# Another order of exponentials and maxima, and work moved away from four places, in a four-layer attention kernel

## The chip, the cores and the metric

The kernel runs on one core of a Trainium2 chip. The core has five engines, each with an instruction stream of its own: TensorE (PE; its weight loads are listed as PEld), VectorE (DVE), ScalarE (ACT), GpSimd (POOL) and SyncE (SP, which here only issues DMAs). Matmul results go to PSUM, which has eight banks of 128 partitions x 512 fp32. The metric is the device time of one execution in microseconds. The kernel before takes 1696.86 us (median of 3 runs, 1695.87 to 1697.17).

## The reference

The input x has 2048 rows of 640. Four layers follow one another in the order A, B, A, B, each with a layernorm ahead of it and a residual around it; both A layers share their weights, and so do both B layers. There are 32 heads of 20. A is linear attention over all rows. B works on four segments of 512 rows: causal softmax attention inside a segment, mixed per head with a read of a memory that earlier segments have filled.

```python
def _A_ref(x, wqkv, wo):
    q, k, v = ...                                   # heads of 20
    phi = lambda t: jnp.where(t > 0, t + 1, jnp.exp(t)) + 1e-6
    pq, pk = phi(q), phi(k)
    kv = jnp.einsum("bhsd,bhse->bhde", pk, v)
    z = jnp.einsum("bhsd->bhd", pk)
    num = jnp.einsum("bhqd,bhde->bhqe", pq, kv)
    den = jnp.einsum("bhqd,bhd->bhq", pq, z)[..., None] + 1e-6
    o = num / den
    return (...)(o) @ wo

def _B_ref(x, wq, wk, wv, wo, beta):
    for s in range(N):                              # 4 segments of 512
        logits = jnp.einsum("bhqd,bhkd->bhqk", qs, ks) * scale + mask
        p = _softmax(logits, axis=-1)
        a_dot = jnp.einsum("bhqk,bhkd->bhqd", p, vs)
        pq = phi(qs)
        num = jnp.einsum("bhld,bhde->bhle", pq, M)
        den = jnp.einsum("bhld,bhd->bhl", pq, z)[..., None] + 1e-6
        a_mem = num / den
        o = g * a_mem + (1.0 - g) * a_dot
        M = M + jnp.einsum("bhld,bhle->bhde", phi(ks), vs)
        z = z + jnp.einsum("bhld->bhd", phi(ks))
    return (...)(o) @ wo
```

## The kernel before, in words

**Two streams.** `run` steps two generators. The dense stream does layernorms, projections, the sums of A and the outputs, for a segment of 512 rows at a time in tiles of 128 rows. The attention stream does the softmax attention of the B layers. Whichever has the lower cost so far goes next. PE executes its instructions in the order in which this program writes them (`MANUAL`). ACT, DVE and POOL are put in order by a scheduler: by priority, which falls as the program goes on and can be raised or lowered for a block (`high_priority`), and with added edges (`issue_after`) that keep an instruction behind another one. Each engine then runs in that order and stops at the first instruction whose inputs are not there.

**Attention.** A unit is four heads of a segment; there are 32 units in a B layer and 64 in all. Every unit passes through three stretches (`STRETCHES`), and a stretch works on up to three units at once: the newest, the one before and the one before that. An entry is an operation, its number and which of these units it belongs to. `max` 0 to 4 (`row_max`) multiplies queries by keys for two banks, after which DVE (L1021) takes the row maxima of each and writes them to `mg`; the banks are free only when DVE is through. `split` turns `mg` into two rows of fp16 (L1030, L1031) that later join the queries, so that the maximum is subtracted by the matmul. `exp` 0 to 4 (`scores`) multiplies keys by queries with those rows for two banks; ACT exponentiates each (L1060, into `pe`) and POOL cuts the causal triangle (L1067). `sum` (`weigh`, L1083) multiplies the exponentials by the values. All of these, and the dense stream too, take their PSUM banks in turn from the same eight.

**The dense stream, where the change touches it.** `opening` starts layer 1: it loads four tiles of x, takes their moments (L350 to L360: statistics on DVE, the power on POOL, `nb` on DVE), normalizes them on ACT (`normed`, L386) and transposes them (`turn`: PE L331, then the lower part through ACT L335 and the upper through DVE L336), while the weights are split into two fp16 parts each (`w_prep`: ACT L271, DVE L272). The weights of the B layers are prepared during layer 1 too; the last of them, `w_Bo`, beside the merge. The merge is the end of the sums of A: DVE scales (L671, L674), PE multiplies (L692), and `wm`, the merged output weight, is formed from L698 to L732. `open_b` opens the buffers of the attention and sets the constant `one` (L841). `a_head` begins the second half of A for a segment (`p_load` reads tiles `pqi` back, `p_read` multiplies and sums them: L764 to L771); `a_second` finishes it, makes the residual x, its moments and the transposed tiles for B. Its `tail` is done later, beside the first value projections of `b_project` (L414, emptied on ACT by `v_half`, L445). `b_out` multiplies by the output weight of B, adds the residual and stores a tile of 128 rows (L982).

```python
L59  [("out", 0, 2), ("exp", 0, 1), ("exp", 1, 1), ("max", 3, 0)],
L60  [("exp", 2, 1), ("exp", 3, 1), ("max", 4, 0), ("split", 0, 0), ("load", 0, 0)]]
```

The other functions named here, and all others that the change touches, follow with their line numbers.

## Time and profile before

| what | value |
|---|---|
| median of 3 runs | 1696.86 us |
| profiled execution | 1699.81 us |
| its span, first to last instruction | 1698.1 us |
| PE busy | 1641.3 us, 97% |
| DVE busy | 1264.6 us, 74% |
| ACT busy | 995.1 us, 59% |
| POOL busy | 505.9 us, 30% |
| PE waiting for DVE's maxima (L1015 for `mg`) | 3.5 us, 6 times |
| DVE waiting for PE before a maximum (L1021) | 41.6 us, 51 times |

The profile is one execution. Its rows come in several views. The page gives each engine's busy time. The view of waits gives an instruction that waited, what it waited for, the total in us, the number of times and the longest. The timeline gives start, duration, engine, line, operation, output <- inputs, shapes and count, and in square brackets the idle time ahead and what ended it. The windows give, for a stretch of time, its length, then the busy time and instructions of PE, weight loads, DVE, ACT and POOL, the mean clock granted to PE (1.00 is full), the share of the DMA engines and their GB/s. Busy times of an engine are no critical path: what ends last in a place is read from the idle times there.

### The profile page before, as it was taken

How to read it: one execution, taken by the hardware profiler on the slowest of the kernel's cores; microseconds unless marked ns; L12 is line 12 of the kernel's file. 1: busy time of each engine (PE TensorE's matmuls, PEld its weight loads, DVE VectorE, ACT ScalarE, POOL GpSimd, SP SyncE). 2: the span in 40 equal slices, each digit the busy share in tenths (PEclk: the TensorE clock that was granted, in tenths of full speed). 3: DMA queues.
4: the chain of work that ended last, by engine and by line, in shares of the span. 5: the costliest groups of instructions: out<-in, count | busy, mean ns of one | idle time of the engine just before them, and what ended most of it. 6: DMA issues, size and time to landing. Idle time of an engine off the chain costs nothing. (4 is left out here: it accounts for less than half of the span.)

```text
span 1698.1 us, 37894 instructions
## 1 busy us (share of the span) xinstructions
PE 1641.3 (97%) x13818; PEld 1021.1 (60%) x13818; DVE 1264.6 (74%) x4015; ACT 995.1 (59%) x1888; POOL 505.9 (30%) x1046
## 2 busy tenths in 40 slices
PE   8999989999999999999999999999999999999998
PEld 6767767564565566556556777766546546645555
DVE  7788886497887787768864566938888888777773
ACT  6666543357657656667665554433675675666763
POOL 4442232022223423433342211210322332232542
PEclk9999999999999999999999999999999999999999
DMA  6415563422312331461211303533232333323422
GB/s 219 156 57 184 214 246 119 148 87 78 114 68 70 127 111 60 134 206 51 80 45 48 108 32 124 191 97 119 76 111 82 104 100 102 106 83 111 148 87 95
DMA packets 110371, 190.99 MB, mean 112 GB/s; under 512 B 14172, under 2 KB 69596, under 8 KB 107624
## 3 DMA queue, kind: packets, MB, share of 16 engines
q1 hardware_dynamic: 97704, 142.68, 26.0%
q0 software_dynamic: 3264, 24.91, 4.1%
q10 hardware_dynamic: 9216, 20.98, 3.2%
q8 instruction: 109, 1.79, 0.4%
q14 instruction: 78, 0.64, 0.1%
HBM read 109.32 MB, written 78.64 MB: 111 GB/s over the span
## 5 line engine op out<-in xcount | busy, mean ns | idle before, releaser
L1021 DVE CUSTOM_DVE_ANT_0 ps<-ps,maskw 128x512 f32<-128x512 f32 (+3 forms) x1024 | 472.1, 521 | 43.8 <-PE ps L1015 41.6
L1060 ACT ACTIVATE pe<-ps,lsc 128x512 f32<-128x512 f32 x640 | 396.7, 696 | 84.5 <-PE ps L1056 82.7
L1067 POOL TENSOR_SCALAR_AFFINE_SELECT pe<-pe 128x256 f32<-128x256 f32 (+1 forms) x640 | 233.3, 372 | 387.6 <-ACT pe L1060 379.6
L414 PEld LDWEIGHTS <-xT 128*128 128x128 f16 x2880 | 280.3, 98 | 112.5 <-issue 6.2
L414 PEld LDWEIGHTS <-oT 128*128 128x128 f16 x1920 | 185.5, 98 | 82.3 <-issue 6.8
L1083 PE MATMUL ps<-pe,v 128*32 128x512 f32 (+3 forms) x2048 | 166.4, 436 | 7.8 <-POOL pe L1067 2.2
L414 PE MATMUL ps<-w_Bo,oT 128*128 128x320 f16 x960 | 143.5, 302 | 3.6 <-ACT oT L335 2.0
L1021 DVE DVE_READ_ACCUMULATOR2_ANT mg<- 128x1 f32 x1024 | 145.2, 142 | 0.0
L590 PE MATMUL ps<-pk,xs 128*128 128x321 f16 (+1 forms) x960 | 138.4, 302 | 4.2 <-DVE pk L553 2.0
L399 PE MATMUL ps<-xT,w_Bq 128*128 128x512 f16 x600 | 140.9, 380 | 1.3 <-ACT pe L1060 0.8
L414 PE MATMUL ps<-wm,oT 128*128 128x320 f16 x960 | 141.0, 299 | 0.5
L414 PE MATMUL ps<-w_Ak,xT 128*128 128x320 f16 x960 | 139.0, 300 | 2.3 <-DVE xT L336 1.6
L414 PE MATMUL ps<-w_Bv,xT 128*128 128x320 f16 x960 | 139.3, 299 | 1.9 <-ACT v L445 1.8
L399 PE MATMUL ps<-xT,w_Bk 128*128 128x512 f16 x600 | 138.5, 379 | 1.2 <-ACT pe L1060 1.2
L414 PE MATMUL ps<-w_Aq,xT 128*128 128x320 f16 x960 | 137.6, 299 | 0.0
L1015 PE MATMUL ps<-ks,qs 60*128 60x512 f16 (+3 forms) x1024 | 123.1, 298 | 8.5 <-DVE mg L1021 3.5
L590 PEld LDWEIGHTS <-xs 128*128 128x128 f16 x960 | 93.2, 98 | 43.6 <-DVE pk L553 2.6
L431 DVE SCALAR_TENSOR_TENSOR e<-e,r 128x320 f32<-128x320 f32 x128 | 67.9, 531 | 67.3 <-ACT r L430 66.9
L1083 PEld LDWEIGHTS ps<-pe,v 128*32 128x32 f32 x2048 | 64.7, 109 | 74.8 <-issue 45.0
L1056 PE MATMUL ps<-qs,ks 62*128 62x128 f16 (+3 forms) x1024 | 105.2, 300 | 1.1 <-ACT pe L1060 1.1
L851 DVE SCALAR_TENSOR_TENSOR nat<-ps,nat 128x512 f16<-128x512 f32 x80 | 55.2, 690 | 64.2 <-ACT nat L850 63.8
L399 PEld LDWEIGHTS <-w_Bk 128*128 128x128 f16 x600 | 57.0, 98 | 66.3 <-issue 6.2
(202 smaller groups left out, 2367.6 us busy)
## 6 DMA issues: line engine op xcount, KB each, us to landing
x<-xn ACTq DMA_DIRECT2D x48, 320.0 KB
qs<-qd SPq DMA_DIRECT2D x128, 120.0 KB
ks<-kd SPq DMA_DIRECT2D x128, 120.0 KB
xo<-x SPq DMA_DIRECT2D x48, 320.0 KB
pqi<-pqd SPq DMA_DIRECT2D x32, 320.0 KB
qd<-nat SPq DMA_DIRECT2D x40, 256.0 KB
kd<-nat SPq DMA_DIRECT2D x40, 256.0 KB
x<-in_A_x SPq DMA_DIRECT2D x16, 320.0 KB
```

The costliest lines, as they stand in the source:

```text
L399: nc.tensor.matmul(p, w[:, c, a, t * P:(t + 1) * P], xT[:, c, b, :], start=k == 0, stop=k == 3 * C - 1)
L414: nc.tensor.matmul(p, xT[:, c, a, i * P:(i + 1) * P], w[:, c, b, n * HN:(n + 1) * HN], start=k == 0, stop=k == 3 * C - 1)
L431: nc.vector.scalar_tensor_tensor(e, e, 1.0, r, op0=OP.min, op1=OP.add)
L590: nc.tensor.matmul(p, xs[:, i, a, c * P:(c + 1) * P], pk[i][:, b, cols], start=i == 0 and a == b, stop=i == NT - 1 and a == 1)
L851: nc.vector.scalar_tensor_tensor(nat[:, 1], p, QK_SHIFT, nat[:, 0], op0=OP.mult, op1=OP.subtract)
L1015: nc.tensor.matmul(bs[par][:, a:a + n], qs[r, p, i * P:(i + 1) * P], ks[r, p, :n], start=True, stop=True)
L1021: nc.vector.tensor_tensor_reduce(bs[par][:, a:a + n], bs[par][:, a:a + n], self.maskw[:, SEG - n:], 1.0, NEG, OP.add, OP.max, G["mg"][:, p ...
L1056: nc.tensor.matmul(b[:, a:a + n], ks[r, p, j * P:(j + 1) * P], qs[r, p, j * P:], start=True, stop=True)
L1060: nc.scalar.activation(e, b, AF.Exp, scale=self.lsc)
L1067: nc.gpsimd.affine_select(d, d, pattern=pat, compare_op=OP.is_ge, fill=0.0, base=0, channel_multiplier=-1)
L1083: nc.tensor.matmul(G["pv"][32 * h4:32 * h4 + 32, j * P:], v[j][:, h * E1:h * E1 + 32], G.pop((p, par, j)), start=j == 0, stop=j == 2, skip ...
```

## The change

It has eight parts.

1. In `STRETCHES`, `max` 3 moves between `exp` 0 and `exp` 1, and `max` 4 with `split` between `exp` 2 and `exp` 3.
2. `exp` 4 gets a higher priority, which counts for ACT and POOL.
3. The DVE half of the split of `w_Bo` gets a lower priority.
4. The constant `one`, and so the buffers of the attention, come after an instruction of the merge (`L["split"]`).
5. In `tail`, the last tile's shift and normalization are written behind the whole first step of the turn before it, and ordered behind the last `v_half` (`self.spread`) as well.
6. In `a_head`, for segments after the first, the load of a tile `pqi` is written one tile ahead of its use.
7. In `opening`, the shift (L355 and L360: `rs`, `nb`) of the last two tiles is ordered behind the lower evacuation of the tile before.
8. The very last tile of the output is stored in two halves of 320 columns.

```diff
-             [("out", 0, 2), ("exp", 0, 1), ("exp", 1, 1), ("max", 3, 0)],
-             [("exp", 2, 1), ("exp", 3, 1), ("max", 4, 0), ("split", 0, 0), ("load", 0, 0)]]
+             [("out", 0, 2), ("exp", 0, 1), ("max", 3, 0), ("exp", 1, 1)],
+             [("exp", 2, 1), ("max", 4, 0), ("split", 0, 0), ("exp", 3, 1), ("load", 0, 0)]]
...
-                self.last = nc.vector.scalar_tensor_tensor(w[:, c, 1, cols], st[:, c, cols], scl, w[:, c, 0, cols],
-                                                           op0=OP.mult, op1=OP.subtract)
+                with self.tc.high_priority(offset=-400) if key == ("B", "o") else nullcontext():
+                    self.last = nc.vector.scalar_tensor_tensor(w[:, c, 1, cols], st[:, c, cols], scl, w[:, c, 0, cols],
+                                                               op0=OP.mult, op1=OP.subtract)
...
-        self.nc.scalar.activation(vv[:, n * HB:(n + 1) * HB, :DH],
-                                  p.rearrange("p (h e) -> p h e", e=DH), AF.Copy, scale=V_SHIFT)
+        self.spread = self.nc.scalar.activation(vv[:, n * HB:(n + 1) * HB, :DH],
+                                                p.rearrange("p (h e) -> p h e", e=DH), AF.Copy, scale=V_SHIFT)
...
-        pq = L["pre"] if s == 0 else [None] * 3
+        pq = L["pre"] if s == 0 else [self.p_load(L, s, 0)]
         box["oT"].append(self.new_oT())
         for i in range(3):
-            yield from self.p_read(L, s, i, box["o"], pq[i])
+            if s > 0 and i < 2:
+                pq.append(self.p_load(L, s, i + 1))
+            yield from self.p_read(L, s, i, box["o"], pq[i], self.nc.vector if s > 0 else None)
...
             t = self.turn(xh[NT - 2], xT, NT - 2)
             yield next(t)
-            with self.tc.issue_after(self.lower.ins):
-                m2 = self.shift(*m)
-            xh.append(self.normed(*m2))
-            yield from t
+            cost = next(t)
+            with self.tc.issue_after(self.lower.ins), self.tc.issue_after(self.spread.ins):
+                xh.append(self.normed(*self.shift(*m)))
+            yield cost
             yield from self.turn(xh[NT - 1], xT, NT - 1)
...
-    def open_b(self):
+    def open_b(self, L):
         self.bp = self.ctx.enter_context(self.tc.tile_pool(name="attn", bufs=1))
-        with self.tc.high_priority():
+        with self.tc.high_priority(), self.tc.issue_after(L["split"].ins):
             self.open_stacks()
...
+                split = st.get("ends") and i == NT - 1
+                if split:
+                    c = slice(n * HN, (n + 1) * HN)
+                    self.q_x.dma_start(dst[s * SEG + i * P:s * SEG + i * P + P, c], xn[:, c])
                 yield self.COST_N
             r = s * SEG + i * P
-            self.q_x.dma_start(dst[r:r + P], xn)
+            if not split:
+                self.q_x.dma_start(dst[r:r + P], xn)
...
                     elif op == "exp":
-                        for bank in EXPS[k]:
-                            self.scores(G, bank)
+                        with self.tc.high_priority(offset=200) if k == 4 else nullcontext():
+                            for bank in EXPS[k]:
+                                self.scores(G, bank)
...
-            m += [self.moments(x[i]) for i in range(2, NT)]
+            m += [self.moments(x[i], False) for i in range(2, NT)]
...
             for i in range(1, NT):
+                if i > 1:
+                    with self.tc.issue_after(self.lower.ins):
+                        m[i - 1] = self.shift(*m[i - 1])
                 xh.append(self.normed(*m[i - 1]))
```

Line numbers of the changed kernel are 1 to 12 higher than those of the one before. How the change moves instructions is shown at three places.

DVE at the first merge. Before, four splits of `w_Bo` stand among the scalings of the merge:

```order
L669 TENSOR_SCALAR eps<-v_83,k_scl 128x1
L272 SCALAR_TENSOR_TENSOR w_Bo<-stage,scl_Bo,w_Bo 128x640 x4
L674 TENSOR_TENSOR xT<-ge,xT 128x320 x2
L671 SCALAR_TENSOR_TENSOR ge<-v_83,eps,rz 128x320
L669 TENSOR_SCALAR eps<-v_84,k_scl 128x1
L669 TENSOR_SCALAR eps<-g_last,k_scl 128x1
L671 SCALAR_TENSOR_TENSOR ge<-v_84,eps,rz 128x320
L674 TENSOR_TENSOR xT<-ge,xT 128x320
```

The fifth follows a little later, and so does the memset of `one` (L841). In the changed kernel, one split stands between the last three L675 (L674 before) of the merge, and the others here, among the instructions that form `wm`:

```order
L770 TENSOR_SCALAR rca<-rca 128x32
L273 SCALAR_TENSOR_TENSOR w_Bo<-stage,scl_Bo,w_Bo 128x640
L771 RECIPROCAL rca<-rca 128x32
L733 SCALAR_TENSOR_TENSOR wm<-ps,wm 128x320 x2
L273 SCALAR_TENSOR_TENSOR w_Bo<-stage,scl_Bo,w_Bo 128x640
L733 SCALAR_TENSOR_TENSOR wm<-ps,wm 128x320 x2
L273 SCALAR_TENSOR_TENSOR w_Bo<-stage,scl_Bo,w_Bo 128x640
L733 SCALAR_TENSOR_TENSOR wm<-ps,wm 128x320 x2
L273 SCALAR_TENSOR_TENSOR w_Bo<-stage,scl_Bo,w_Bo 128x640
L733 SCALAR_TENSOR_TENSOR wm<-ps,wm 128x320
L844 MEMSET one 2x1024
L733 SCALAR_TENSOR_TENSOR wm<-ps,wm 128x320
```

Four splits and the memset have moved from ahead of the merge's last scalings to between the `wm` instructions.

ACT in the opening. Before, the last two tiles are normalized one right behind the other (L386 x2):

```order
L386 ACTIVATE xh<-x,nb,rs 128x640 x2
L428 ACTIVATE e<-ps,inv_Ak 128x320
L430 ACTIVATE r<-ps,inv_Ak 128x320
L335 ACTIVATE xT<-ps 128x3x128
L335 ACTIVATE xT<-ps 128x2x128
L566 ACTIVATE pk<-e,k_scl 128x320
L497 ACTIVATE xs<-xh 128x640
L335 ACTIVATE xT<-ps 128x3x128
```

After the change (line numbers one higher):

```order
L387 ACTIVATE xh<-x,nb,rs 128x640
L429 ACTIVATE e<-ps,inv_Ak 128x320
L431 ACTIVATE r<-ps,inv_Ak 128x320
L336 ACTIVATE xT<-ps 128x3x128
L336 ACTIVATE xT<-ps 128x2x128
L567 ACTIVATE pk<-e,k_scl 128x320
L498 ACTIVATE xs<-xh 128x640
L387 ACTIVATE xh<-x,nb,rs 128x640
L336 ACTIVATE xT<-ps 128x3x128
```

The second normalization has moved behind six instructions of the tile before.

DVE in the third stretch of a unit, beside `p_read`. Here the maxima (each an ISA row that reduces and one that reads the result into `mg`) stand before behind the multiply of `pqi`:

```order
L894 TENSOR_TENSOR acc<-ps,acc 128x63
L336 TENSOR_TENSOR oT<-ps,oT 128x3x128
L749 TENSOR_TENSOR mem_80<-acc,blk 32x2x63
L764 TENSOR_TENSOR pqi<-pqi,z 128x640
L1021 ISA ps,mg<-ps,maskw 128x256
L1021 ISA mg 128x1
L1021 ISA ps,mg<-ps,maskw 128x256
L1021 ISA mg 128x1
```

After the change (L764 is L765 there, L1021 is L1029):

```order
L337 TENSOR_TENSOR oT<-ps,oT 128x3x128
L750 TENSOR_TENSOR mem_80<-acc,blk 32x2x63
L1029 ISA ps,mg<-ps,maskw 128x256
L1029 ISA mg 128x1
L1029 ISA ps,mg<-ps,maskw 128x256
L1029 ISA mg 128x1
L1029 ISA ps,mg<-ps,maskw 128x256
L1029 ISA mg 128x1
L1029 ISA ps,mg<-ps,maskw 128x256
L1029 ISA mg 128x1
L765 TENSOR_TENSOR pqi<-pqi,z 128x640
```

The multiply has moved behind the four maxima of `max` 4.

More of the change, by code (lines that the diff above doesn't have):

```diff
@@ L755, in p_load, with p_read @@
         return pq
-    def p_read(self, L, s, i, o, pq=None):
+    def p_read(self, L, s, i, o, pq=None, eng=None):
         nc = self.nc
-        eng = nc.gpsimd
+        eng = eng or nc.gpsimd
         if pq is None:
@@ L1271, in dense @@
         stage_ctx.close()
-        self.open_b()
+        self.open_b(L)
         i = 0
```

## The prediction

> **What bounds the kernel now.** I read the page first: which engine fills the span, and at what clock.
>
> ```profile
> span 1698.1 us, 37894 instructions
> PE 1641.3 (97%) x13818; PEld 1021.1 (60%) x13818; DVE 1264.6 (74%) x4015; ACT 995.1 (59%) x1888; POOL 505.9 (30%) x1046
> ```
>
> TensorE (PE) is the bound. The change removes no matmul, so all it can win is PE's idle time, 1698.1 − 1641.3 = 56.8 us, and time at half clock. The next view is therefore the waits of PE by what ended them (total us, times, longest):
>
> ```profile
> PE ps L1015 <- DVE mg L1021: 3.5, 6, 0.8
> ...
> PE ps L692 <- DVE xT L674: 2.3, 5, 0.6
> ...
> PE ps L1083 <- POOL pe L1067: 2.2, 7, 0.6
> ...
> PE ps L399 <- ACT pe L1060: 2.0, 5, 0.4
> PE ps L1015 <- ACT pe L1060: 2.0, 5, 0.6
> ...
> PE ps L414 <- ACT v L445: 1.8, 2, 0.9
> PE ps L414 <- DVE xT L336: 1.6, 1, 1.6
> ```
>
> The idle time is in many small pieces, so each part of the change can win a few us at most. The profiled execution took 1699.81 us, 1.71 more than its span; the median of the runs is 1696.86, 2.95 lower. I sum against 1699.81 and carry the difference over to the median.
>
> **The first merge (weight splits L272, `one` L841).** The windows compare the first merge (layer 1) with the second (layer 3), then the phase behind the first that forms `wm`. Columns: length, then busy time and instructions of PE, weight loads, DVE, ACT, POOL, then the clock.
>
> ```profile
> 233.30:247.90 14.60, 10.38 (x107) 8.52 (x105) 14.38 (x39) 6.38 (x15) 1.80 (x6) 0.81 0.61 232
> 1070.40:1077.20 6.80, 6.80 (x108) 6.20 (x106) 6.72 (x19) 3.86 (x10) 0.92 (x3) 1.00 0.19 56
> 247.90:257.70 9.80, 9.80 (x80) 5.33 (x78) 7.19 (x20) 4.02 (x11) 4.84 (x5) 0.94 0.77 276
> ```
>
> In the first merge DVE is busy 14.38 of 14.60 us: it is the bound there, not PE. The timeline shows what stands on DVE beside the merge:
>
> ```profile
> 228.91 3.26 DVE L272 SCALAR_TENSOR_TENSOR w_Bo<-stage,scl_Bo,w_Bo 128x640 f16<-128x640 f32 x4
> ...
> 236.13 0.88 DVE L272 SCALAR_TENSOR_TENSOR w_Bo<-stage,scl_Bo,w_Bo 128x640 f16<-128x640 f32 x1
> ...
> 237.63 0.91 DVE L841 MEMSET one<- 2x1024 f16 x1
> ```
>
> In the new order one L272 stays ahead of the last two L674 and four go between the L732 of the `wm` phase, with the memset ahead of the last. So 4 x 0.82 (3.26/4) + 0.91 = 4.2 us leave the merge, which ends that much earlier. In the `wm` phase DVE then has 7.19 + 4.2 = 11.4 us of work for a stretch of 9.80: 1.6 us come back, since the matmuls behind need the last `wm`. Net −2.6; ends −4.2 (all of it finds room) and 0 (all comes back).
>
> The clock bears on this place and on the opening. Windows of 3.4 us, busy PE and clock as above:
>
> ```profile
> 17.10:20.50 3.40, 3.01 (x19) 1.67 (x17) 3.40 (x10) 3.36 (x8) 0.00 (x0) 1.00 0.30 122
> 20.50:23.90 3.40, 1.49 (x10) 0.90 (x11) 2.43 (x11) 3.17 (x7) 2.69 (x5) 0.99 1.06 358
> 23.90:27.30 3.40, 3.40 (x16) 2.66 (x15) 1.60 (x4) 2.28 (x6) 2.35 (x8) 0.50 0.61 211
> 27.30:30.70 3.40, 3.40 (x27) 2.54 (x26) 2.02 (x5) 2.67 (x7) 2.20 (x2) 1.00 0.91 293
> ```
>
> ```profile
> 239.00:242.40 3.40, 1.78 (x27) 1.26 (x26) 3.40 (x9) 1.92 (x4) 1.08 (x4) 0.99 0.75 312
> 242.40:245.80 3.40, 2.32 (x20) 1.95 (x20) 3.33 (x10) 2.62 (x7) 0.34 (x1) 0.50 0.85 265
> 245.80:249.20 3.40, 3.40 (x25) 2.87 (x24) 2.42 (x8) 0.44 (x2) 1.14 (x4) 0.51 0.96 391
> ```
>
> A window with PE busy 1.49, 1.78 or 2.32 us is followed by one at half clock; one with 3.01 or 3.40 is not. In 245.8–249.2 PE is full at half clock, so without that dip up to 1.7 us more would go. PE's work in the merge would be spread over some 10.4 instead of 14.6 us, near 2.4 us a window, too close to 2.32 to count on; I leave the 1.7 to a rival. The Trainium skill ("TensorE: Matmul & The Clock Gate", What's actually happening) says the clock halves after an idle window of about 3.4 us and returns after a busy one, in windows that run free of the kernel. The half clock and the return agree with the trace; that the window must be idle does not, since 1.49 busy us were enough. By the page no dip would be left to lose or to win here, and the sum would lack the opening's 1.7 us below.
>
> **The opening (moments of the last two tiles).** PE waits 1.63 us for DVE's L336, ahead of which two `nb` (L360) wait for POOL:
>
> ```profile
> 21.55 0.21 DVE L360 TENSOR_SCALAR nb<-mv,rs 128x1 f32<-128x1 f32 x1 [0.44 <-POOL rs L355]
> ...
> 22.77 1.73 ACT L386 ACTIVATE xh<-x,nb,rs 128x640 f32<-128x640 f32 x2
> 22.86 2.72 PE L414 MATMUL ps<-w_Ak,xT 128*128 128x320 f16 x13 [1.63 <-DVE xT L336]
> ...
> 25.37 1.92 PE L331 MATMUL ps<-ident,xh 128*128 128x128 f32 x8
> 25.61 0.53 ACT L428 ACTIVATE e<-ps,inv_Ak 128x320 f32<-128x320 f32 x1 [1.12 <-PE ps L414]
> ...
> 27.08 2.30 PE L414 MATMUL ps<-w_Ak,xT 128*128 128x320 f16 x15
> ...
> 27.59 0.72 ACT L497 ACTIVATE xs<-xh 128x640 f16<-128x640 f32 x1
> ```
>
> The change takes the `nb`, their waits and so some 0.65 us (0.44 + 0.21) away from L336. L414 then runs mostly ahead of 23.9, where the clock halves, and its 13 end some 1.5 us earlier. But the L386 of the last tile, now side by side with the one before (x2 at 22.77), goes behind six ACT instructions, L428 to L497, which take 28.31 − 25.61 = 2.7 us. From 24.1 (25.61 − 1.5) that makes 26.8, and with its own 0.87 (half of 1.73) 27.7; I say 28.0, since the L335 among the six wait for transposes at half clock. PE's transposes of both tiles follow one another (L331 x8), so the last three wait for it, and L414 starts about 28.35: +1.3. In 23.9–27.3 PE would then be busy about 1.9 us, less than 2.32, and the next window falls to half clock: another 1.7. I take +2.0, because some of that dip would stand beside waits; ends −0.7 (only L336 counts) and +3.0.
>
> **The tail of a segment.** A PE wait of 0.92 stands at 1193.43, its twin of 0.93 in the first B layer (the row of 1.8 us, 2 times, above):
>
> ```profile
> 1192.14 0.92 ACT L386 ACTIVATE xh<-xn,nb,rs 128x640 f32<-128x640 f32 x1 [0.75 <-DVE nb L360]
> ...
> 1192.96 0.42 ACT L445 ACTIVATE v<-ps 128x320 f32<-128x320 f32 x1
> ...
> 1193.43 1.79 PE L414 MATMUL ps<-w_Bv,xT 128*128 128x320 f16 x12 [0.92 <-ACT v L445]
> ```
>
> ACT waits 0.75 for `nb`, normalizes for 0.92, and only then empties the bank that PE needs. Behind the change L445 comes first, so both waits go: −1.8. Late next is the normalized tile itself, some 1 us later; its transposes stand behind a dozen L414 (1.79 us), which cover most of it; I give back 0.4. Taken −1.4; ends −1.8 and +0.5.
>
> **Exponential 4 first on ACT.** Its two activations now stand together and ahead of evacuations that stood before or between them. The longest of the seven waits of L1083 for POOL:
>
> ```profile
> 902.31 0.57 ACT L430 ACTIVATE r<-ps,inv_Ak 128x320 f32<-128x320 f32 x1
> ...
> 902.72 1.31 ACT L1060 ACTIVATE pe<-ps,lsc 128x512 f32<-128x512 f32 x2
> ...
> 904.24 0.99 PE L1083 MATMUL ps<-pe,v 128*32 128x256 f32 x8 [0.63 <-POOL pe L1067]
> ```
>
> L430 goes behind, so 0.41 (902.72 − 902.31) of the 0.63 goes here. Of the 2.2 us in all I count a little over half: −1.2; ends −2.2 and +1.5, since `r` comes 1.3 us later in some units, and DVE's L431 behind it, though no matmul is near (taken at 0).
>
> **Maxima between the exponentials.** On DVE the four maxima of stretch 3 now stand ahead of the multiply L764, which waits for a DMA:
>
> ```profile
> 1264.62 0.92 DVE L764 TENSOR_TENSOR pqi<-pqi,z 128x640 f32<-128x640 f32 x1 [0.94 <-DMA pqi<-pqd]
> ...
> 1266.76 1.03 PE L1015 MATMUL ps<-ks,qs 60*128 60x512 f16 x5 [0.63 <-DVE mg L1021]
> ```
>
> The other such place has 1.21 of DVE and 0.80 of PE. Both PE waits should go: −1.4. Elsewhere the maxima reach PE one pair of exponentials earlier (128 places, two in each of 64 units) and that pair as much later. How long a pair is, and how DVE stands to PE:
>
> ```profile
> 362.56 0.61 PE L1056 MATMUL ps<-qs,ks 62*128 62x384 f16 x8
> ```
>
> ```profile
> DVE ps L1021 <- PE ps L1015: 41.6, 51, 3.3
> ```
>
> The eight matmuls are two pairs, so 0.3 us each. Only 51 times did DVE wait for PE before a maximum; mostly it is behind, and a maximum that comes 0.3 us early meets its bank that much less free. Against it, ACT gets four activations in two bursts instead of one, and PE's waits for `pe` (2.0 + 2.0 above) lie where ACT is behind. I set these two against each other: taken −1.5 for the whole part; ends −4 (those waits gone as well) and +10 (the first rival). The new order of the loads of `pqi` on SP's queue differs at two places only: 0.
>
> **The end.** The last output leaves in two halves:
>
> ```profile
> 1694.35 0.55 DVE L493 SCALAR_TENSOR_TENSOR xn<-ps,ioB,xo 128x320 f32<-128x320 f32 x1 [1.49 <-PE ps L414]
> ```
>
> DVE ends at 1694.90, the span at 1698.1: 3.2 us of issue, packets and closing. Only packets shrink, by half: −0.4; ends −0.8 and 0 (one more issue).
>
> Sum: −2.6 + 2.0 − 1.4 − 1.2 − 1.5 − 0.4 = −5.1. 1699.81 − 5.1 = 1694.7 in a profiled execution, and 1696.86 − 5.1 = 1691.8 as a median (−0.30%). What a measurement of this kernel tells from no change is about 0.2%, 3.4 us.
>
> **Rivals.**
> - Slower: the maxima come too early for their banks. At 0.3 us a place, a quarter of the 128 places costs 32 x 0.3 = 9.6 us. The other parts give −3.6, so 1696.9 − 3.6 + 9.6 = 1702.9. It decides for slower from 23 places on (7.0/0.3). For it: DVE is mostly behind PE. Against: only 3.5 us of waits for `mg` today, in 6 places, and PE was only 0.3 us away from the earlier place. Chance 0.22.
> - No change: the gains are hidden. DVE is full in the merge and nearly in the `wm` phase, so the splits only change places (0); tail and exponential 4 give half (−0.7, −0.6); maxima 0; opening +2.0; end −0.4: 1696.9 + 0.3 = 1697.2. Chance 0.27.
> - More: the dip at 242–249 vanishes (−1.7) and the bursts on ACT, halved, take the 4.0 us of waits for `pe` down by 2.5: 1691.8 − 4.2 = 1687.6. Chance 0.13.
> - My forecast, 1688.5 to 1693.4: 0.38.
>
> Faster is forecast and "more", 0.51; same 0.27; slower 0.22. The range 1684.5 to 1702 leaves out the upper half of the first rival and a tenth below.
>
> **What would show it.** In the profile after: DVE's L272 no longer in the merge, the merge's window about 10.4 us; a PE wait for L386 near 26–28 us and half clock behind it; no L414 wait for `v` L445; less than 1.2 us of L1083 waiting for POOL; L1015 waiting for `mg` below 3.5 us. The last row alone, if it grew to 10 us, or new waits of L1056 for `pe`, would make the prediction wrong.

## The result and the profile after

The changed kernel takes 1682.84 us (median of 4 runs, 1681.48 to 1685.04) against 1696.36 us before (4 runs): a ratio of 0.9922, 95% interval 0.9909 to 0.9934. That is 13.5 us faster, where 5.1 were forecast and 1684.5 was the lower end of the range. The direction was right and the size was not.

The page of the changed kernel, its span and its engines:

```profile
span 1681.9 us, 37873 instructions
...
PE 1625.1 (97%) x13818; PEld 1018.3 (61%) x13818; DVE 1262.9 (75%) x4015; ACT 994.8 (59%) x1888; POOL 505.5 (30%) x1046
```

This line is the key to everything below. PE's idle time is 1681.9 − 1625.1 = 56.8 us, the same as before (1698.1 − 1641.3). The 16.2 us between the two spans came out of PE's *busy* time, although its 13818 matmuls are the same. So the sum in the prediction, which counted idle time, looked in the wrong column for most of the gain. (Part of the 16.2 us is half clock in the execution profiled before; the last section counts it.)

Waits of PE after, for the places that the prediction spoke of:

```profile
PE ps L415 <- DVE oT L337: 5.2, 6, 3.4
PE ps L332 <- ACT xh L387: 3.8, 3, 2.7
PE ps L1091 <- POOL pe L1075: 3.3, 2, 1.7
...
PE ps L693 <- DVE xT L675: 0.9, 1, 0.9
```

The merge's wait for `xT` (L692 before, 2.3 us) has shrunk, the wait of the value projection for `v` L445 (1.8) is gone, and the maxima's wait for `mg` (3.5) with it. New are a wait of 3.4 us for `oT` behind the merge, 2.7 us in the opening, and two of 1.7 us at the sums.

### The profile page after: what moved, and what is told of

Same layout as the page of the kernel before. It is cut to its first block, busy times and chain, and to the rows that moved or that the text cites. A ratio compares the mean times of both kernels' runs of the same rounds, so it can differ in the third digit from the quotient of the medians.

```text
span 1681.9 us, 37873 instructions
## 1 busy us (share of the span) xinstructions
PE 1625.1 (97%) x13818; PEld 1018.3 (61%) x13818; DVE 1262.9 (75%) x4015; ACT 994.8 (59%) x1888; POOL 505.5 (30%) x1046
## 4 chain that ended last, share of the span: by engine, by line
PE 72%; DVE 14%; ACT 8%; DMA 3%; issue 2%; SPq 1%; POOL 1%; ACTq 0%; DVEq 0%; POOLq 0%
PE ps L415 30%; PE ps L400 13%; PE ps L1091 8%; PE ps L591 5%; PE ps L1064 4%; PE ps L332 4%; PE ps L1023 3%; ACT pe L1068 3%; DVE ps L1029 2%; PE ps L468 2%; PE ps L1104 1%; DVE e L432 1%; DVE wmx L245 1%; DVE nat L854 1%; DVE pk L554 1%
## 5 line engine op out<-in xcount | busy, mean ns | idle before, releaser
L1029 DVE CUSTOM_DVE_ANT_0 ps<-ps,maskw 128x384 f32<-128x384 f32 (+3 forms) x1024 | 472.7, 520 | 32.3 <-PE ps L1023 28.1
L415 PEld LDWEIGHTS <-xT 128*128 128x128 f16 x2880 | 280.7, 98 | 110.5 <-issue 4.5
L415 PEld LDWEIGHTS <-oT 128*128 128x128 f16 x1920 | 185.3, 98 | 87.3 <-issue 7.8
L1091 PE MATMUL ps<-pe,v 128*32 128x512 f32 (+3 forms) x2048 | 157.2, 436 | 9.8 <-POOL pe L1075 3.3
L415 PE MATMUL ps<-wm,oT 128*128 128x320 f16 x960 | 142.7, 301 | 4.8 <-DVE oT L337 4.4
L415 PE MATMUL ps<-w_Bo,oT 128*128 128x320 f16 x960 | 141.5, 299 | 3.8 <-ACT oT L336 2.0
L1029 DVE DVE_READ_ACCUMULATOR2_ANT mg<- 128x1 f32 x1024 | 143.8, 140 | 0.1
L415 PE MATMUL ps<-w_Ak,xT 128*128 128x320 f16 x960 | 139.7, 301 | 1.6 <-DVE xT L337 0.9
L415 PE MATMUL ps<-w_Bv,xT 128*128 128x320 f16 x960 | 139.3, 299 | 0.1
L415 PE MATMUL ps<-w_Aq,xT 128*128 128x320 f16 x960 | 137.6, 299 | 0.0
L1064 PE MATMUL ps<-qs,ks 62*128 62x512 f16 (+3 forms) x1024 | 129.5, 299 | 3.6 <-ACT pe L1068 2.2
L1023 PE MATMUL ps<-ks,qs 60*128 60x512 f16 (+3 forms) x1024 | 115.8, 297 | 2.3 <-ACT pe L1068 1.1
L336 ACT ACTIVATE oT<-ps 128x384 f16<-128x384 f32 (+1 forms) x128 | 55.9, 445 | 71.7 <-PE ps L332 54.3
```

The lines of the kernel that those rows point to most:

```text
L415: nc.tensor.matmul(p, xT[:, c, a, i * P:(i + 1) * P], w[:, c, b, n * HN:(n + 1) * HN], start=k == 0, stop=k == 3 * C - 1)
L1023: nc.tensor.matmul(bs[par][:, a:a + n], qs[r, p, i * P:(i + 1) * P], ks[r, p, :n], start=True, stop=True)
L1029: nc.vector.tensor_tensor_reduce(bs[par][:, a:a + n], bs[par][:, a:a + n], self.maskw[:, SEG - n:], 1.0, NEG, OP.add, OP.max, G["mg"][:, p ...
L1064: nc.tensor.matmul(b[:, a:a + n], ks[r, p, j * P:(j + 1) * P], qs[r, p, j * P:], start=True, stop=True)
L1091: nc.tensor.matmul(G["pv"][32 * h4:32 * h4 + 32, j * P:], v[j][:, h * E1:h * E1 + 32], G.pop((p, par, j)), start=j == 0, stop=j == 2, skip ...
```

## Experiments

All were timed against the kernel before on the same chip; "ratio" is to that kernel.

| kernel | median us | ratio, 95% interval |
|---|---|---|
| changed kernel | 1682.84 | 0.9922 (0.9909 to 0.9934) |
| before + new order of maxima | 1694.80 | 0.9995 (0.9984 to 1.0006) |
| before + priority of exponential 4 | 1685.64 | 0.9944 (0.9929 to 0.9959) |
| before + priority of its first activation only | 1697.21 | 1.0005 (0.9993 to 1.0017) |
| before + sum 2 written later | 1694.64 | 0.9991 (0.9981 to 1.0000) |
| before + priority + new tail | 1679.90 | 0.9908 (0.9890 to 0.9926) |
| changed − priority of exponential 4 | 1694.59 | 0.9984 (0.9971 to 0.9996) |
| changed − new order of maxima | 1683.02 | 0.9917 (0.9897 to 0.9936) |
| changed, maxima first in both stretches | 1695.75 | 0.9996 (0.9986 to 1.0007) |
| changed − edge ahead of `one` | 1683.43 | 0.9931 (0.9916 to 0.9946) |
| changed − late splits and edge | 1683.01 | 0.9922 (0.9904 to 0.9940) |
| changed − new opening | 1680.85 | 0.9913 (0.9898 to 0.9928) |
| changed − new tail | 1686.65 | 0.9943 (0.9921 to 0.9964) |
| changed − new opening − new order | 1677.77 | 0.9894 (0.9879 to 0.9909) |
| the same, priority on all exponentials | 1681.10 | 0.9916 (0.9897 to 0.9934) |

### Which of the two large parts it is

My first theory after seeing the result was that both the order of the maxima and the priority had been undervalued. The rival was that only one of them had.

The order of the maxima alone:

```diff
-             [("out", 0, 2), ("exp", 0, 1), ("exp", 1, 1), ("max", 3, 0)],
-             [("exp", 2, 1), ("exp", 3, 1), ("max", 4, 0), ("split", 0, 0), ("load", 0, 0)]]
+             [("out", 0, 2), ("exp", 0, 1), ("max", 3, 0), ("exp", 1, 1)],
+             [("exp", 2, 1), ("max", 4, 0), ("split", 0, 0), ("exp", 3, 1), ("load", 0, 0)]]
```

> The kernel before with the new order of exponentials and maxima in the two stretches, and nothing else of the change. Theory A (the maxima's PSUM banks: before, PE loses time at the maxima that the list of waits shows under several names, 8.5 us in all and some more inside time that counts as busy; mixing exponentials and maxima removes it): 8 to 11 us faster than before, median about 1687, the idle time ahead of the maxima's matmuls from 8.5 to under 3 us. Theory B (the forecast was right on this part, and the gain beyond it comes from the exponentials' priority or from both together): 1 to 3 us faster, 1694 to 1696.

Measured: 1694.80 against 1696.12, ratio 0.9995. Theory A falls. The groups of PE's matmuls show why. First the page of the kernel before (busy us, mean ns of one, then the idle time ahead and what ended it):

```profile
L1083 PE MATMUL ps<-pe,v 128*32 128x512 f32 (+3 forms) x2048 | 166.4, 436 | 7.8 <-POOL pe L1067 2.2
...
L1015 PE MATMUL ps<-ks,qs 60*128 60x512 f16 (+3 forms) x1024 | 123.1, 298 | 8.5 <-DVE mg L1021 3.5
...
L1056 PE MATMUL ps<-qs,ks 62*128 62x128 f16 (+3 forms) x1024 | 105.2, 300 | 1.1 <-ACT pe L1060 1.1
```

And the same groups with the new order alone, from the view by line:

```profile
L1083 PE MATMUL ps<-pe,v 128*32 128x512 f32 (+3 forms) x2048 | 169.1, 437 | 10.2 <-POOL pe L1067 3.4 <-ACT r L440 1.3 <-DVE oT L336 1.2
L1056 PE MATMUL ps<-qs,ks 62*128 62x512 f16 (+3 forms) x1024 | 129.7, 299 | 4.1 <-ACT pe L1060 2.2 <-DVE xT L336 0.6 <-ACT r L430 0.5
L1015 PE MATMUL ps<-ks,qs 60*128 60x512 f16 (+3 forms) x1024 | 115.5, 297 | 2.3 <-DVE oT L336 1.6 <-ACT pe L1060 0.5
```

The idle time ahead of the maxima (L1015) fell from 8.5 to 2.3 us, just as theory A said. But the idle time ahead of the exponentials' matmuls (L1056) rose from 1.1 to 4.1, and ahead of the sums (L1083) from 7.8 to 10.2. That is −6.2 + 3.0 + 2.4 = −0.8 us. What PE saves at one bank it pays at the next. The busy times of these two groups cannot be compared between the orders: a group's busy time counts only its own matmuls, and with maxima between the exponentials L1056 rises from 105.2 to 129.7 us at the same count and mean, though the kernel is no slower.

The priority alone:

```diff
-                        for bank in EXPS[k]:
-                            self.scores(G, bank)
+                        with self.tc.high_priority(offset=200) if k == 4 else nullcontext():
+                            for bank in EXPS[k]:
+                                self.scores(G, bank)
```

> The kernel before with the priority of exponential 4 and nothing else. Theory A (each late piece of exponential 4 costs PE more than its idle time, because the matmuls of the four heads, which otherwise run side by side, then start one after the other): 5 to 9 us faster, 1688 to 1692, with the waits of the sums for POOL below 2 us apart from two new ones in the first segments. Theory B (only the idle time shown counts): 1 to 2 us faster, 1695 to 1696.

Measured: 1685.64, 0.56% or 9.5 us faster than before. Theory A holds, with its size a little exceeded. The two new waits that it expected in the first segments did not come: the sums wait for POOL once, for 0.5 us. (The two of 1.7 us in the changed kernel need the new tail and the new order of the maxima together: without the tail there is one of 0.5 us, with the old order two of at most 0.6.) The group of the sums with the priority alone:

```profile
L1083 PE MATMUL ps<-pe,v 128*32 128x512 f32 (+3 forms) x2048 | 156.9, 436 | 6.5 <-ACT pe L1060 2.1 <-DVE acc L894 1.0 <-DVE m L1031 1.0
```

Same 2048 matmuls, same mean of 436 ns, but 156.9 us busy instead of 166.4: −9.5. Busy time is the time in which at least one matmul runs, and matmuls of several heads run side by side; how far they do decides it. One unit shows it in the timeline. Before:

```profile
610.50 0.68 ACT L438 ACTIVATE e<-ps,inv_Bk 128x512 f32<-128x512 f32 x1
...
611.07 0.69 ACT L440 ACTIVATE r<-ps,inv_Bk 128x512 f32<-128x512 f32 x1
...
611.41 1.51 PE L1083 MATMUL ps<-pe,v 128*32 128x384 f32 x18
611.64 0.70 ACT L1060 ACTIVATE pe<-ps,lsc 128x512 f32<-128x512 f32 x1
...
613.15 0.63 PE L1083 MATMUL ps<-pe,v 128*32 128x256 f32 x6 [0.24 <-POOL pe L1067]
```

The same unit with the priority alone:

```profile
605.89 1.27 ACT L1060 ACTIVATE pe<-ps,lsc 128x512 f32<-128x512 f32 x2 [0.31 <-PE ps L1056]
...
607.38 1.51 PE L1083 MATMUL ps<-pe,v 128*32 128x384 f32 x24
```

With the second activation late behind L438 and L440, the 24 matmuls of three sums take from 611.41 to 613.78, 2.37 us. With both in time they take 1.51. The loss is 0.86 us, of which the profile calls 0.24 idle: the last six matmuls, which otherwise run beside others, stand as busy time of their own. In the unit at 656 us the whole loss is hidden: 24 matmuls take 2.32 us before and 1.74 with the priority, with no idle time ahead of the last sum in either row. The granted clock was 1.00 around both units.

```profile
655.84 2.32 PE L1083 MATMUL ps<-pe,v 128*32 128x384 f32 x24
```

```profile
650.55 1.74 PE L1083 MATMUL ps<-pe,v 128*32 128x384 f32 x24
```

All 64 units together: from the first start to the last end of these 24 matmuls it is 111.1 us in the trace of before and 99.8 with the priority, 11.3 less. Before, 15 units take more than 2 us, with the priority two.

Both parts, taken out of the whole one at a time:

```diff
-                        with self.tc.high_priority(offset=200) if k == 4 else nullcontext():
+                        with nullcontext():
```

> The changed kernel without the priority of exponential 4. Theory A (that priority is the gain, and the rest of the change is worth 2 to 4 us): 8 to 11 us slower than the changed kernel, 1691 to 1694. Theory B (the parts overlap, so that another part has the same gain): less than 5 us slower, under 1688.

Measured: 1694.59. Without the priority, 0.9984 − 0.9922 = 0.62% or 10.5 us are lost; with all its other parts the change is 0.16% faster than before (interval 0.04 to 0.29%), some 2.7 us. Theory A.

The old order of the maxima in the changed kernel (the first diff among the experiments the other way round):

> The changed kernel with the old order of exponentials and maxima in both stretches, all else as changed. Theory A (the new order takes waits from the maxima but gives as much to what follows them, as it did alone): within 2 us of the changed kernel, 1681 to 1685. Theory B (the new order pays once exponential 4 has priority): 4 to 8 us slower than the changed kernel, 1687 to 1691.

Measured: 1683.02, ratio 0.9917 against 0.9922. The order of the maxima does nothing in the whole either: theory A.

### What it is about the priority

Two activations make up exponential 4, and each carries two of the four heads. Only the first gets the priority:

```diff
-                        for bank in EXPS[k]:
-                            self.scores(G, bank)
+                        for b, bank in enumerate(EXPS[k]):
+                            with self.tc.high_priority(offset=200) if k == 4 and b == 0 else nullcontext():
+                                self.scores(G, bank)
```

> The kernel before with the priority on the first of the two activations of exponential 4 alone. Theory A (sum 2 needs both pieces; what counts is the end of the second, and pieces that come apart make the heads' matmuls run in two groups): at most 3 us faster than before, 1693 to 1697, and the busy time of the sums' matmuls at 163 us or more (166.4 before, 156.9 with the full priority). Theory B (the first activation coming earlier is what pays, for instance because it frees its bank): at least half of the full priority's gain, 5 us or more, 1691 or less.

Measured: 1697.21, ratio 1.0005: nothing is left of the gain. The sums:

```profile
L1083 PE MATMUL ps<-pe,v 128*32 128x512 f32 (+3 forms) x2048 | 165.6, 436 | 8.8 <-POOL pe L1067 2.6 <-ACT pe L1060 1.8 <-DVE acc L894 1.0
```

165.6 us busy, about as before the change, and 16 units with more than 2 us for their 24 matmuls. So the first piece alone gains nothing, and the end of the second counts: theory A. No run has the priority on the second alone.

The other way to make sum 2 wait less is to ask for it later:

```diff
-              ("sum", 2, 2), ("copy", 0, 2), ("max", 2, 0)],
+              ("max", 2, 0), ("sum", 2, 2), ("copy", 0, 2)],
```

> The kernel before, in which the last sum of a unit (sum 2, the one that reads exponential 4) and the copy behind it are written behind the maximum 2, and nothing else. ACT's order of priorities is left alone; PE has the two matmuls of the maximum (some 0.4 us) to do before it needs the late exponentials. Theory A (the loss is PE's lateness at this sum, whose matmuls run one by one when the exponentials come in pieces): 3 to 7 us faster than before, 1689 to 1693. Theory B (the gain of the priority comes from somewhere else, for instance the evacuations behind it on ACT): no gain, 1695 to 1698.

Measured: 1694.64, ratio 0.9991 with an upper end of 1.0000: about 1.5 us at most, which neither theory had. The wait for POOL falls from 2.2 to 0.8 us, but the busy time is not better:

```profile
L1083 PE MATMUL ps<-pe,v 128*32 128x512 f32 (+3 forms) x2048 | 172.0, 438 | 6.1 <-DVE acc L894 1.0 <-DVE m L1031 1.0 <-ACT r L440 0.9
```

172.0 us against 166.4. A maximum between sums 3 and 2 keeps the last eight matmuls of every unit from running beside those ahead of them, so what lateness cost in some units the new order costs in all. That is how I read the 172.0, and it is not shown: a group's own busy time also grows when other matmuls are put between its own, as at L1056 above. This run does not decide between the theories by itself.

### Where a maximum stands

```diff
-             [("out", 0, 2), ("exp", 0, 1), ("max", 3, 0), ("exp", 1, 1)],
-             [("exp", 2, 1), ("max", 4, 0), ("split", 0, 0), ("exp", 3, 1), ("load", 0, 0)]]
+             [("out", 0, 2), ("max", 3, 0), ("exp", 0, 1), ("exp", 1, 1)],
+             [("max", 4, 0), ("split", 0, 0), ("exp", 2, 1), ("exp", 3, 1), ("load", 0, 0)]]
```

> The changed kernel with the maxima ahead of both exponentials of their stretch (maximum 3, exponentials 0 and 1; maximum 4, split, exponentials 2 and 3). Theory A (the place of a maximum among the exponentials hardly matters, since what PE saves at its banks it pays at the next): within 2 us of the changed kernel. Theory B (it is the alternation of banks for DVE and for ACT that pays; with the maxima first PE waits for them, and four banks in a row then wait for ACT): 4 us or more slower than the changed kernel.

Measured: 1695.75, which is 12.9 us slower than the changed kernel. Theory B. So the place matters on one side only: between the exponentials or behind both is the same, ahead of both is bad. The waits with the maxima first:

```profile
PE ps L1091 <- ACT pe L1068: 3.5, 10, 0.7
PE ps L400 <- ACT pe L1068: 2.8, 5, 0.6
...
PE ps L1091 <- ACT r L441: 2.5, 5, 0.8
...
PE ps L332 <- ACT pe L1068: 2.0, 4, 0.6
```

All four rows are waits for ACT, which gets its four activations later: the sums' wait for `pe` rose from 2.4 (6 times) to 3.5 (10 times). Waits for `mg` did not come back (0.5 us once, 0.4 in the changed kernel), so the half of theory B that has PE wait for the maxima is wrong. This time the loss lies in idle time, as the page shows:

```profile
span 1692.6 us, 37857 instructions
...
PE 1625.4 (96%) x13818; PEld 1015.1 (60%) x13818; DVE 1258.2 (74%) x4015; ACT 993.5 (59%) x1888; POOL 507.7 (30%) x1046
```

PE is busy as long as in the changed kernel (1625.4 and 1625.1 us) and idle for 67.2 us instead of 56.8: 10.4 of the 10.7 us between the two spans. Most of it ends with ACT; DVE's evacuations have a share too (L415 for `oT` 7.0 us instead of 5.2).

### The merge

The constant `one` without the new edge, then also the splits back in their place:

```diff
-        with self.tc.high_priority(), self.tc.issue_after(L["split"].ins):
+        with self.tc.high_priority():
```

> The changed kernel with the constant `one` set early again (no edge behind the merge); the weight splits stay late. Theory A (the late constant holds back the merged weight's last instruction, and its six copies on SP's queue stand ahead of the loads of the residual, for which DVE then waits 5.1 us): 2 to 4 us faster than the changed kernel, 1679 to 1681, no wait of DVE for the residual at 265 to 270 us. Theory B (the splits alone fill DVE, the constant only adds its 0.9 us): at most 1 us faster, 1682 to 1683.

Measured: 1683.43, no gain (0.9931), and DVE's wait for the residual is still there (5.9 us). Theory A falls, and for a reason that is in the order of instructions: the memset stands at the same place without the edge, behind the last split. The buffers of the attention are opened after the staging buffers of the weights are closed, so they wait for the last reader of those, which is the split. The run measured a difference that was not there.

```diff
-                with self.tc.high_priority(offset=-400) if key == ("B", "o") else nullcontext():
+                with nullcontext():
```

> The changed kernel with the weight splits of w_Bo and the constant `one` where they were before the change. Theory A (the merge gets shorter by as much as the phase behind it gets longer): within 1.5 us of the changed kernel, 1681 to 1684. Theory B (the forecast: 2.6 us lost): 1685 to 1687.

(with the edge taken away as well). Measured: 1683.01, ratio 0.9922, the same as the changed kernel. Theory A: the moved work gains nothing. The windows of the changed kernel that answer to the merge and the `wm` phase, and the one behind them, in the columns of the prediction:

```profile
237.60:245.90 8.30, 7.24 (x107) 6.37 (x106) 8.30 (x21) 4.13 (x11) 1.46 (x6) 1.00 0.06 22
245.90:255.10 9.20, 9.20 (x81) 5.06 (x79) 9.20 (x26) 4.60 (x13) 5.25 (x6) 1.00 0.88 299
255.10:264.30 9.20, 5.77 (x31) 3.70 (x31) 7.59 (x15) 2.05 (x6) 1.87 (x2) 0.81 0.92 303
```

The merge takes 8.3 us instead of 14.6 and the `wm` phase 9.2 instead of 9.8. DVE is full in both (8.30 of 8.30, 9.20 of 9.20). Its debt falls due in the third window, where PE is busy for 5.77 of 9.20 us:

```profile
258.30 0.91 DVE L844 MEMSET one<- 2x1024 f16 x1 [0.16 <-DVE wm L733]
259.24 3.73 SPq L847 DMA_DIRECT2D ks<-one  x6
...
260.07 3.45 PE L415 MATMUL ps<-wm,oT 128*128 128x320 f16 x13 [3.40 <-DVE oT L337]
...
263.01 7.91 SPq L343 DMA_DIRECT2D xo<-in_A_x  x4
...
269.90 1.01 DVE L494 SCALAR_TENSOR_TENSOR xn<-ps,ioG,xo 128x320 f32<-128x320 f32 x2 [5.11 <-DMA xo<-in_A_x]
```

PE waits 3.40 us for an evacuation that stands behind the splits, the memset and the last `wm` on DVE. SP's queue has the six copies of `one` ahead of the loads of the residual, as it had before the change; but the copies need the memset, and that is late now. With the splits and the memset in their old place the copies start at 243.47 us and the loads at 248.90, and DVE does not wait for the residual; here the loads start at 263.01, so that DVE waits 5.11 us for `xo` at 269.90 with PE's next evacuation behind it.

How the gain is given back can be counted, because PE has the same order in both kernels. The first transpose behind the `wm` phase (L332) starts at 255.10 us here and at 262.87 with the old place, 7.8 us later (0.7 of this is older than the merge). The transpose that stands 149 matmuls behind it starts at 281.31 and 282.92, so 1.6 us are left, 0.9 without the 0.7. Half clock has a part in both: in the gain two stretches of 3.4 us that only the old place has (247.8 to 254.6), in the loss one that only the new place has (260.3 to 263.7).

### The opening and the tail

The opening as before (no shift behind the lower evacuation):

```diff
-            m += [self.moments(x[i], False) for i in range(2, NT)]
+            m += [self.moments(x[i]) for i in range(2, NT)]
...
-                if i > 1:
-                    with self.tc.issue_after(self.lower.ins):
-                        m[i - 1] = self.shift(*m[i - 1])
```

> The changed kernel with the opening as before. Theory A (the wait of 2.7 us for the last tile's normalization at 28 us is the loss, and nothing behind hides it): 2.5 to 3.2 us faster than the changed kernel, about 1680. Theory B (the loss is hidden by a later wait, for weights that come by DMA in the first 120 us): within 1 us of the changed kernel.

Measured: 1680.85, 2 us below the changed kernel; the intervals of the ratios overlap (0.9898 to 0.9928 and 0.9909 to 0.9934), so the times alone leave it unclear. The traces are clearer: PE's 501st matmul starts at 80.83 us in the changed kernel, at 78.16 with the old opening and at 77.94 before the change. The trace of the changed kernel has the wait:

```profile
27.07 0.91 ACT L387 ACTIVATE xh<-x,nb,rs 128x640 f32<-128x640 f32 x1
28.02 0.76 PE L332 MATMUL ps<-ident,xh 128*128 128x128 f32 x3 [2.71 <-ACT xh L387]
28.58 0.47 PE L415 MATMUL ps<-w_Ak,xT 128*128 128x320 f16 x1
```

The tail as before:

```diff
-            cost = next(t)
-            with self.tc.issue_after(self.lower.ins), self.tc.issue_after(self.spread.ins):
-                xh.append(self.normed(*self.shift(*m)))
-            yield cost
+            with self.tc.issue_after(self.lower.ins):
+                m2 = self.shift(*m)
+            xh.append(self.normed(*m2))
+            yield from t
```

> The changed kernel with the tail of a segment as before (the last tile is normalized ahead of the value projection's evacuation). Theory A (the two waits of 0.9 us come back, about 1.1 us each from start to start, and 0.5 each of new waits goes): 1 to 2.5 us slower than the changed kernel, 1684 to 1685.5. Theory B (the gain of the tail is given back before the segment ends): within 1 us.

Measured: 1686.65, 0.9943 − 0.9922 = 0.21% or 3.6 us slower (intervals 0.9921 to 0.9964 and 0.9909 to 0.9934, which just overlap). More than theory A had.

The kernel before with two parts only, the priority and the new tail (the diff above the other way round):

> The kernel before with the priority of exponential 4 and the new tail, and nothing else. Theory A (these two parts are all of the change that pays; the rest is neutral, and the opening costs 2 to 3 us): 1 to 4 us faster than the changed kernel, 1679 to 1682. Theory B (the loads of pqi, the merge or the output's end carry the rest of the gain): 1684 or more.

Measured: 1679.90, ratio 0.9908: theory A, and 2.9 us below the changed kernel. Against the priority alone (0.9944, 0.9929 to 0.9959) the tail brings 0.36% or 6.1 us, with intervals that do not touch. So it does more than remove the two waits for `v`. With the priority alone, this row stands high in the list of waits:

```profile
PE pm L1039 <- ACT pe L1060: 2.2, 4, 0.6
```

With priority and tail together it reads:

```profile
PE pm L1039 <- ACT pe L1060: 0.7, 2, 0.4
```

In four units (at 499, 651, 1321 and 1455 us in the trace of the priority alone) the last tile's normalization, 0.92 us on ACT, stood ahead of exponential 4 and so ahead of everything that PE takes its banks from; the new tail puts it behind. I had counted the two units in which it stood ahead of `v` and not these four. The tail also takes four of the six waits of the maxima for `mg`, which stand 13 to 17 us behind the two for `v`; I had looked at `mg` under the maxima only. With the priority alone, then with both:

```profile
PE ps L1015 <- DVE mg L1021: 3.0, 6, 0.6
```

```profile
PE ps L1015 <- DVE mg L1021: 0.5, 2, 0.3
```

These rows are 1.8 us (`v`), 1.5 (`pe`) and 2.5 (`mg`), 5.8 in all, against 1.7 of new waits: PE's idle time falls from 55.5 to 51.4 us.

### A faster kernel

The changed kernel with the old opening and the old order of the maxima (their diffs above, together):

> The changed kernel with the old opening and the old order of exponentials and maxima. Theory A (the first costs 2 to 3 us in the changed kernel, the second nothing): 1 to 3 us faster than the changed kernel, 1679 to 1682. Theory B (both matter in the other direction when taken together): 1683 or more.

Measured: 1677.77 (four runs within 0.6 us), ratio 0.9894, interval 0.9879 to 0.9909: faster than before, and about 5 us below the changed kernel, whose interval (0.9909 to 0.9934) it just touches. That is more than the two parts gave one at a time (2.0 and −0.2 us). Part of it may be the clock: up to 120 us its profile has no half clock, that of the changed kernel two stretches of 3.4 us (28.2 to 31.6 and 117.0 to 120.4). No run shows why the two together give more.

The same with the priority on all five exponentials:

```diff
-                        with self.tc.high_priority(offset=200) if k == 4 else nullcontext():
+                        with self.tc.high_priority(offset=200) if True else nullcontext():
```

> As the kernel with the old opening and the old order, and with the priority on all five exponentials. Theory A (only sum 2 needs its exponentials at once; the others are needed a stretch later, and ACT's other work is late instead): 0 to 4 us slower than that kernel. Theory B (PE's waits for the banks of exponentials, about 8 us under `pe` in the list of waits, shrink as well): 2 to 5 us faster than it.

Measured: 1681.10, 3.3 us slower than without (the intervals overlap a little, 0.9897 to 0.9934 and 0.9879 to 0.9909; the four times of each do not). Theory A by its time: the priority pays for the one exponential that is read at once, not for those that have a stretch to spare. Why it costs was not looked into; PE's idle time is 53.3 us instead of 50.9, its busy time the same.

## Why the prediction was wrong, point by point

- **Exponential 4: the term that was mis-sized.** The step was "of the 2.2 us in all I count a little over half: −1.2; ends −2.2 and +1.5". It measured −9.5 us alone and −10.5 in the whole. The mechanism was right (evacuations between and ahead of the two activations make the last sum late), but the end of the range was set by the idle time in the list of waits, which holds a small part of the loss. The rest is busy time of matmuls that run one group after the other, 166.4 − 156.9 = 9.5 us in the group of L1083. The account had shut this out in its first step, "all it can win is PE's idle time, 1698.1 − 1641.3 = 56.8 us, and time at half clock": the busy time of the same matmuls can shrink too. The rows to see it were in the trace of before: units with 24 matmuls in 1.51 us beside others with 2.32 or 2.37. The sign that was named, "less than 1.2 us of L1083 waiting for POOL", did not come in the changed kernel (3.3 us in two waits) and was no measure of the gain.
- **The tail: right, and too small.** −1.4 was forecast from two waits for `v`; −3.6 to −6.1 us were measured: four more units had the same normalization ahead of exponential 4, and four waits for `mg` went with it.
- **The merge: wrong in its balance.** −2.6 was forecast, 0 measured. The merge and the `wm` phase together gained more than I had (24.4 us before, 17.5 after), but I stopped the account at the last `wm`. The evacuations behind it wait for DVE, and the residual's loads come 14 us later on SP's queue (263.01 instead of 248.90), which I did not follow here; of the 7.1 us gained by the end of the `wm` phase, 0.9 are left 149 matmuls on. The edge ahead of `one`, which I counted as a moved memset of 0.9 us, moves nothing by itself.
- **The maxima: nearly right as a sum.** −1.5 forecast, −0.8 ± 1.9 measured alone and nothing in the whole. The waits for `mg` did go; others came. My rival, that a maximum 0.3 us earlier costs 0.3 us at a quarter of the places, did not come in this order. A loss of that size came when both maxima were put first, +12.9 us, but mostly at the banks of ACT, not at those of the maxima.
- **The opening: the wait right, the clock by luck.** Transposes at 28.0 and L414 at 28.35 were forecast, with +1.3 for the wait and +2.0 with the clock; they came at 28.02 and 28.58, and the opening as before is 2.0 us faster, with overlapping intervals. By the traces the price is 2.9 us against the kernel before. Half clock does follow the wait (28.2 to 31.6 us), but in this execution the earlier stretch, 23.9 to 27.3 before the change, is missing, so the mean clock over 20 to 36 us is 0.89 in both. In four other kernels with the new opening (without the priority, without the merge's part, without the tail, and with the maxima first) both stretches came, and it is 0.79.
- **The end: right.** From the end of the last L494 (1678.65 + 0.55) to the end of the span are 2.7 us instead of 3.2: −0.5 for a forecast of −0.4. No run tested it alone, nor the earlier loads of `pqi`.

The three terms with the largest errors (exponential 4, tail, merge) sum to −5.2 in the forecast and to about −13 to −17 in the runs; the measured whole, −13.5, lies there. The rest of the account is smaller than what the runs can tell.

## What to carry to other kernels

Idle time is not the whole price of a late operand. Where several small matmuls normally overlap, compare the time of such a group in a unit that is on time with one that is late, and multiply the difference by the number of late units; the total busy time of a group whose count and mean do not change is the check, as long as its order among the other matmuls does not change either. And when work is moved out of a full stretch, follow every engine and queue that it holds back until the debt is paid, not only to the end of the phase where it lands.

## What the hardware showed that was not expected

The half clock of PE is partly a matter of chance. The kernel before and the one with old opening and old order have nearly the same work in two stretches, and the profile of each shows about the same busy time, but not the same clock (the column ahead of the last two). Before:

```profile
20.00:31.00 11.00, 8.76 (x54) 6.32 (x53) 6.84 (x21) 8.92 (x19) 7.25 (x13) 0.84 0.86 291
108.00:120.00 12.00, 9.37 (x58) 5.85 (x56) 9.03 (x16) 5.03 (x11) 6.40 (x8) 0.86 0.15 55
```

With old opening and old order:

```profile
20.00:31.00 11.00, 8.99 (x67) 6.66 (x68) 8.47 (x22) 10.41 (x22) 9.06 (x15) 1.00 0.90 312
108.00:120.00 12.00, 9.14 (x66) 6.10 (x64) 9.73 (x21) 6.69 (x13) 4.82 (x7) 1.00 0.11 41
```

The same idle stretch halved the clock in one execution and not in the other. The Trainium skill ("TensorE: Matmul & The Clock Gate", What's actually happening) says that the windows run free of the kernel, which agrees. Each stretch of 3.4 us at half clock costs up to 1.7 us (half of 3.4), and single executions of the kernel before lay between 1691.9 and 1700.7 us, with a mean granted clock of 1.000 and 0.995. So a profiled execution may stand some us off the median: the one before was at 1699.81. Part of the 16.2 us between the two profiles is such a dip (1638 to 1645 us in the first, none in the second), and only the timed ratios say what a part is worth.

That idle time of PE can stay the same to 0.1 us while 16 us go was the second surprise. The group of the sums has 9.2 us less busy time in the changed kernel (166.4 and 157.2). PE was busy for 17.8 us at half clock in the profile of before and for 10.2 in that of the changed kernel; if work at half clock takes twice as long, that is another 3.8, an estimate. The last 3.2 of the 16.2 us stay open. The idle time did not fall because new waits took the place of those that went (the list in the first section).
